# Moving the staging places of the second and fourth group of Q, K, V rows into the third slot of keys

## The chip, the cores and the metric

One core of a Trainium2 chip. The metric is the device time of one execution in microseconds (us), the median of several runs. The engines are TensorE (PE, whose weight loads are shown as PEld), VectorE (DVE), ScalarE (ACT), GpSimd (POOL) and SyncE (SP). SP, ACT and POOL also issue DMA transfers.

## What is computed

A transformer block of 2048 tokens of width 576, attention and feed-forward side by side on the same normalized input:

```python
qkv = (lambda x, *d: x.transpose(*d))((x @ wqkv).reshape(B, S, 3, H, Dh), 2, 0, 3, 1, 4)
...
logits = jnp.einsum("bhsd,bhswd->bhsw", q, kg) * scale
logits = jnp.where(mask[None, None, :, :], logits, -1e9)
attn = _softmax(logits, axis=-1)
o = jnp.einsum("bhsw,bhswd->bhsd", attn, vg)
return (lambda x, *d: x.transpose(*d))(o, 0, 2, 1, 3).reshape(B, S, D) @ wo
...
h = jnp.einsum("bsd,df->bsf", x, w1) + b1
r = jnp.where(h > zero, h, zero)
h = r * r
out = jnp.einsum("bsf,fd->bsd", h, w2) + b2
...
xn = _layernorm(x, axis=-1)
return x + _A_ref(xn, A_wqkv, A_wo) + _B_ref(xn, B_w1, B_b1, B_w2, B_b2)
```

There are 32 heads of 18, and a token attends to 8 places: itself and seven before it, two apart (kg and vg are the keys and values there). The feed-forward goes from 576 to 4608 and back.

## The kernel before

The tokens are four blocks (b = 0 to 3) of 512. All matrix products are in fp32, with each operand split into a high and a low part (ACT copies the high part, DVE subtracts it to get the low one). In order of the program:

- `open_rows` normalizes block 0, turns it and multiplies it by the weights of head group 0 (groups g = 0 to 3, 8 heads each). Four products of 128 tokens ("rows", j = 0 to 3) come out, each 128x432: K, V and Q of one group.
- `q0` computes the 28 remaining rows of blocks 0 and 1, in the order (0,1), (0,3), (0,2), (1,3), (1,2), (1,1), (1,0) as (block, group), four rows each. **Row r** below is the r-th of these, r = 0 to 27. Rows 0 to 25 run here, the last two inside the next stage. Between rows, `run(pieces, k)` issues pieces of other work: statistics and normalization of block 1 (`normalize`), the sums of blocks for the fast matrix scheme of the feed-forward (`sums`), the splitting of the next groups' weights (`split_wq`), small left-over weights (`left_w`, with the ACT copy L589), and then steps of attention (`side`).
- `phase_a(0)` begins the feed-forward of blocks 0 and 1. Its first product (L676) needs the first half of the first weights, which ACT copies (`w1_hi`, L514) and DVE finishes (`w1_lo`), after DVE has combined them (`combine_w1`). Then feed-forward, the rows of blocks 2 and 3, and the second feed-forward follow.

**A row's way.** `qkv_row` (L361 on) takes PSUM bank r % 5, PE multiplies 14 times (L365), and `qkv_out` (L356 on) has ACT copy the bank into a place of the staging tile `st` (L357); ACT itself then issues the transfer of the place to a buffer in DRAM (`kvq`, L359). `st` has four places, one for each j, so row r copies into the place of row r-4, and the copy waits until that row's transfer has landed.

**Slots of keys.** A pool called `kv` has three buffers ("slots"), taken in rotation; a tile waits until the last user of its slot is done. At the start they hold the rows of block 0, the rows of block 1 and the normalized rows. Then attention's keys and values live there: `fetch` (L374 on) loads them when `free[0]`, the count of free slots, exceeds `kept_back[0]`. Here one slot is kept back while the keys and values of (0,0) are loaded after row 6, and given after row 17 to `load_left_x(0, ...)`: two small loads on SP (L599) of left-over inputs. Behind them in SP's queue stand three loads of second weights (`load_w2`, L535) and the next first weights (`load_w1`, L499, L501).

**Order.** The program is written out by hand; each engine executes its own instructions in that order. A DMA instruction whose counters have not been reached holds up everything behind it on the issuing engine. Eight counters (DMAHW0 to 7 below) are raised when transfers of SP and ACT land; they are handed out in turn, and a transfer that gets a counter waits until the one that had it before has landed.

Of the kernel before, what the change touches and what calls it, by code (L numbers as in the profile page):

```python
# [11 lines left out]
AF = mybir.ActivationFunctionType  # L12
# [9 lines left out]
NJ = TB // P  # L22
# [5 lines left out]
CG = HG * DH  # L28
QW = 3 * CG
# [21 lines left out]
def block_kernel(ctx: ExitStack, tc: tile.TileContext, x, xt, wqkv, wo, w1, b1, w2, b2, w1l, out):  # L51
    nc = tc.nc
# [12 lines left out]
    def kv_tile(n):  # L65
        return sb.tile([P, n], F32, name="kv", bufs=3)
# [47 lines left out]
    def bank(i):  # L114
        return ps.tile([P, TB], F32, name=f"p{i}")
# [53 lines left out]
    def statistics(b):  # L169
        mr = sb.tile([P, 2, NJ], F32, name="mr")  # L170
        for j in range(NJ):
            for k in range(2):
                if b == 1:
                    bn_stats(b, rows_of[b], j, k)
                else:
                    if k == 0:
                        ln[b, j] = sb.tile([P, 2, 6], F32, name="st6", bufs=NJ)
                    nc.vector.bn_stats(out=ln[b, j][:, k], in_=rows_of[b][j][:, 0, k * 288:(k + 1) * 288])
            mean_var(b, j)
            nc.vector.tensor_copy(mr[:, 0, j:j + 1], ln[b, j][:, 0:1])  # L180
            inverse_std(mr[:, 1, j:j + 1], ln[b, j][:, 1:2])
            if j == NJ - 1:
                if b > 1:
                    nc.gpsimd.dma_start(mrscr[b].rearrange("n p -> p n"), mr.rearrange("p k j -> p (k j)"))
                mrs[b] = mr
                measured.add(b)
                if b == 1:
                    release()
            yield
# [12 lines left out]
    def turn_mr(b, i):  # L202
        y = bank(i)
        nc.tensor.transpose(y[:2 * NJ, :P], mrs[b].rearrange("p k j -> p (k j)"), ident)
        t = sb.tile([2 * NJ, P], F32, name="mrt")
        nc.scalar.activation(t, y[:2 * NJ, :P], AF.Copy)
        nc.sync.dma_start(mrscr[b], t)

    def load_mb(b):
        assert b in measured  # L210
        mb[b] = (sb.tile([P, 2, TB], F32, name="mb") if b < 3 else
                 sb.tile([P, 2 * NS * P], F32, name="st")[:, :2 * TB].rearrange("p (k t) -> p k t", k=2))
        nc.sync.dma_start(mb[b].rearrange("c k t -> c (k t)"), flat(mrscr[b], 0, [0, P], 2 * NJ * P))
# [13 lines left out]
    def normalize(b):  # L227
        open_x(b)
        for a in (0, 2):
            v = xm[b][:, a:a + 2]  # L230
            for k, op in enumerate((ALU.subtract, ALU.mult)):
                tt(v, v, mb[b][:, k:k + 1].to_broadcast([P, 2, TB]), op)
                if k:
                    soon(lambda v=v, a=a: nc.scalar.activation(X[b][:, 0, a:a + 2], v, AF.Copy))
                yield
        for k, op in enumerate((ALU.subtract, ALU.mult)):
            tt(xf[b], xf[b], mb[b][:, k], op)
        nc.sync.dma_start(xlscr[b], xf[b][:2 * L])
        soon(lambda: left_hi(x4[b], xf[b]))
        yield  # L240
        for a in (0, 2):
            flush()
            tt(X[b][:, 1, a:a + 2], xm[b][:, a:a + 2], X[b][:, 0, a:a + 2].bitcast(F32), ALU.subtract)
            yield
        flush()
        left_lo(x4[b], xf[b])
        normed.add(b)
        yield
# [60 lines left out]
    def load_wq(g, ks=range(3)):  # L309
        for k in ks:  # L310
            n = 2 if k < 2 else 1
            r = raws[g, k] = sb.tile([P, 2, QW], F32, name="r4", bufs=4)[:, :n]
            nc.sync.dma_start(r, wqkv[g, :, 2 * k:2 * k + n])
# [14 lines left out]
    def split_wq(g, name, then=lambda: None):  # L328
        open_wq(g, name)
        for k in range(4):  # L330
            if k < 3:
                wq_hi(g, k)
            if k:
                wq_lo(g, k - 1)
                if k == 3:
                    then()
                    split_up.add(g)
                yield

    qp, stage = {}, {}  # L340

    def row_products(b, g, j):
        js = slice(j * P, (j + 1) * P)
        mm = []
        for c in range(NC):
            w = wq[g, c // 2][:, c % 2]
            if c < NC - 1:
                mm += [(X[b][:, 0, c, js], w[:, 0]), (X[b][:, 1, c, js], w[:, 0]), (X[b][:, 0, c, js], w[:, 1])]
            else:
                mm += [(x4[b][:, js], w[:, 0]), (x4[b][:, js], w[:, 1])]  # L350
        return mm
# [1 line left out]
    def open_stage():  # L353
        stage[0] = sb.tile([P, 2 * NS * P], F32, name="st")[:, :NJ * QW].rearrange("p (j c) -> p j c", c=QW)

    def qkv_out(b, g, j, p):  # L356
        nc.scalar.activation(stage[0][:, j], p[:, :QW], AF.Copy)  # L357
        to = kvq[g][:, PAD + b * TB:PAD + (b + 1) * TB].rearrange("i (p j) c -> p j i c", j=NJ)[:, j]
        nc.scalar.dma_start(to, stage[0][:, j].rearrange("p (i c) -> p i c", c=CG))  # L359

    def qkv_row(b, g, j, i):  # L361
        p = bank(i)
        mm = row_products(b, g, j)
        for k, (l, r) in enumerate(mm):
            nc.tensor.matmul(p[:, :QW], l, r, start=k == 0, stop=k == len(mm) - 1)  # L365
        qkv_out(b, g, j, p)

    def shifted(t, j, *dims):
        a = t[:, j:j + 1, 0:1]
# [2 lines left out]
    loads, landed, queue, free, lane, kept_back = [], {}, [], [0], [nc.sync], [0]  # L372
# [21 lines left out]
    def offer(b, g=None):  # L394
        if g is None:
            loads.append(("x", b, None))
            queue.append((("x", b), lambda: statistics(b)))
        else:
            loads.extend([("k", b, g), ("v", b, g)])
            queue.append((("k", b, g), lambda: attention(b, g)))  # L400
        fetch()
# [77 lines left out]
    def run(gens, k):  # L479

        flush()
        while k > 0 and gens:
            try:
                next(gens[0])
                k -= 1
            except StopIteration:
                gens.pop(0)
        side(k)
# [134 lines left out]
    def load_left_w(i, v):  # L623
        rv["w", i] = v
        nc.sync.dma_start(v[:, :4], w1l[i])
# [687 lines left out]
    def run_all(gens):  # L1313
        while gens:
            run(gens, 1)
# [239 lines left out]
    def q0():  # L1555
        todo = [(b, g, j) for b, g in ((0, 1), (0, 3), (0, 2), (1, 3), (1, 2), (1, 1), (1, 0)) for j in range(NJ)]
        pieces = [statistics(1), split_wq(3, "S")]

        waiting = []

        def row(r):
            b, g, j = todo[r]
            while b and b not in normed or g not in split_up:
                run(pieces, 1)
            qkv_row(b, g, j, r % 5)
            if j == NJ - 1:
                def go(b=b, g=g):
                    offer(b, g)

                if r < 6:  # L1570
                    waiting.append(go)
                else:
                    go()

        for r in range(len(todo) - 2):
            row(r)
            if r == 2:
                turn_mr(1, 7)
                run_all(pieces)
                load_wq(2)  # L1580
                load_mb(1)
            if r == 1:
                load_left_w(0, sb.tile([P, 2 * NS, P], F32, name="w1r", bufs=2))
            if r == 4:
                pieces += [split_wq(2, "h", lambda: load_wq(0)), normalize(1), left_w(0)]
            if r == 6:
                offer(0, 0)
                for late in waiting:
                    late()
                waiting.clear()  # L1590
                lane[0] = nc.gpsimd
            if r == 11:
                run_all(pieces)
                load_w1(0)
            if r == 13:
                pieces.append(sums(0))
            if r == 17:
                free[0] -= 1
                kept_back[0] = 0
                load_left_x(0, kv_tile(2 * NS * P).rearrange("p (s t) -> p s t", t=P))  # L1600
            if r == 19:
                split_up.discard(0)
                pieces.insert(0, split_wq(0, "h"))
            if r == 21:
                run_all(pieces)
                for n in range(3):
                    load_w2(n)
                combine_w1(0)
                load_w1(1)
            if r in (23, 24):  # L1610
                w1_hi(0, r - 23)
                w1_lo(0, r - 23)
            elif r not in (3, 22):
                run(pieces, 3 if r < 1 or 14 <= r < 20 else 1 if r > 20 else 2)

        def filler(i):
            if i < 2:
                row(len(todo) - 2 + i)
            if i == 1:
                last_sum(0)  # L1620

        return filler
# [73 lines left out]
```

## Time and profile before

| | |
|---|---|
| median of 3 runs | 1102.7 us (1102.13 to 1104.84) |
| the profiled execution's own time | 1102.89 us |
| its span, first to last instruction | 1101.2 us |
| PE busy | 1093.1 us, 99% |
| DVE, ACT, POOL busy | 879.5, 562.2, 149.0 us |
| granted TensorE clock | 1.000 |

The times are one execution's, in us from the span's start. In rows of the timeline the columns are: start, duration, engine, line, operation, output<-input, shape, count, and in brackets the idle time just ahead and what the profile takes to have ended it. "ACTq" and "SPq" are DMA instructions on those engines' queues. Matmul ends are modelled, so their starts are the better measure.

### The profile page before, as it was taken

To read this page: it belongs to the slowest core of one execution; us is meant where nothing else is said; L and a number is where in the kernel's file an instruction comes from. 1 tells how busy PE (TensorE), PEld (TensorE's weight loads), DVE (VectorE), ACT (ScalarE), POOL (GpSimd) and SP (SyncE) were. 2 spreads that over 40 slices of the span, in tenths; PEclk is the share of its full clock that TensorE was granted. 3 is DMA by queue.
4 is the path that set the end of the run, shared out by engine and by line. 5 is a ranking of instruction groups with operands and counts; after the bars stand their busy time and mean duration, and the time that the engine had idled before them with its cause. 6 is when DMAs were issued, how large, how long until landed. Compare 5 with 4: busy or idle time off the path is not lost.

```text
span 1101.2 us, 13948 instructions
## 1 busy us (share of the span) xinstructions
PE 1093.1 (99%) x4936; PEld 923.2 (84%) x4936; DVE 879.5 (80%) x1183; ACT 562.2 (51%) x794; POOL 149.0 (14%) x267
## 2 busy tenths in 40 slices
PE   9999999999999999999999999999999999999998
PEld 7998888888888888888899988888888888888887
DVE  7596988899898978999879387776767676889955
ACT  5435766656566654555344345454554545543432
POOL 4000401022030101003010300201101010101010
PEclk9999999999999999999999999999999999999999
DMA  7956998879989887869565988868686877685572
GB/s 278 329 188 233 344 384 320 330 269 272 377 328 299 301 331 255 299 233 328 201 212 164 305 313 300 299 232 318 215 304 210 293 241 298 219 291 190 184 284 88
DMA packets 109558, 298.97 MB, mean 271 GB/s; under 512 B 12648, under 2 KB 42736, under 8 KB 98608
## 3 DMA queue, kind: packets, MB, share of 16 engines
q1 hardware_dynamic: 69984, 192.84, 49.8%
q0 software_dynamic: 13200, 62.52, 16.0%
q10 hardware_dynamic: 26304, 42.71, 11.8%
q8 instruction: 39, 0.64, 0.2%
q14 instruction: 31, 0.25, 0.1%
HBM read 213.53 MB, written 84.50 MB: 271 GB/s over the span
## 4 chain that ended last, share of the span: by engine, by line
PE 94%; DVE 3%; DMA 1%; issue 1%; ACT 1%; ACTq 0%; POOL 0%; DVEq 0%; POOLq 0%
PE p L572 47%; PE p L676 35%; PE p L1102 6%; PE p L365 3%; PE p L1106 1%; PE p L1471 1%; DMA kvq<-st 1%; PE p L682 1%; DVE w1r L118 1%; DVE pr L118 0%; PE p L1388 0%; DVE r L118 0%; DVE S L118 0%; DVE w1s L118 0%; ACT st L357 0%
## 5 line engine op out<-in xcount | busy, mean ns | idle before, releaser
L572 PE MATMUL p<-h,w2s 128*128 128x512 f32 x2066 | 491.3, 389 | 0.1
L572 PEld LDWEIGHTS p<-h,w2s 128*128 128x128 f32 x2066 | 387.5, 188 | 81.4 <-ACT h L722 0.6
L676 PE MATMUL p<-X,w1s 128*128 128x512 f32 x864 | 219.6, 389 | 2.1 <-DVE w1s L118 1.3
L676 PEld LDWEIGHTS p<-X,w1s 128*128 128x128 f32 x864 | 162.0, 188 | 36.3 <-DVE w1s L118 1.7
L545 ACT ACTIVATE w2s<-w2r 128x640 fp32r<-128x640 f32 x164 | 120.2, 735 | 126.5 <-PE p L572 102.1
L118 DVE TENSOR_TENSOR w2s<-w2r,w2s 128x576 fp32r<-128x576 f32 x164 | 123.5, 753 | 72.4 <-ACT w2s L545 72.1
L676 PE MATMUL p<-S,w1s 128*128 128x512 f32 x648 | 164.5, 389 | 0.0
L676 PEld LDWEIGHTS p<-S,w1s 128*128 128x128 f32 x648 | 121.5, 188 | 25.2
L443 POOL DMA_DIRECT2D o<-q x128 | 69.3, 609 | 416.7 <-DVE q L118 415.1
L718 ACT ACTIVATE r<-r,b1t 128x512 f32<-128x512 f32 x72 | 52.2, 725 | 116.4 <-DVE r L118 115.4
L414 DVE TENSOR_REDUCE lg<-pr 128x64 f32<-128x1152 f32 x64 | 86.5, 1351 | 1.2
L118 DVE TENSOR_TENSOR pr<-lg,kv 128x1152 f32<-128x1152 f32 x64 | 86.7, 1354 | 1.0
L118 DVE TENSOR_TENSOR pr<-q,kv 128x1152 f32<-128x1152 f32 x64 | 86.6, 1354 | 0.9
L118 DVE TENSOR_TENSOR pr<-pr 128x576 f32<-128x576 f32 (+1 forms) x128 | 77.6, 606 | 3.5
L118 DVE TENSOR_TENSOR r<-p,r 128x512 f32<-128x512 f32 (+1 forms) x77 | 53.1, 689 | 32.8 <-ACT r L784 15.3
L726 ACT ACTIVATE r<-r 128x1024 f32<-128x1024 f32 x72 | 76.1, 1057 | 1.2
L118 DVE TENSOR_TENSOR h<-r,h 128x1024 fp32r<-128x1024 f32 (+3 forms) x46 | 51.7, 1135 | 23.2 <-ACT r L726 14.9
L760 ACT ACTIVATE r<-p 128x512 f32<-128x512 f32 x36 | 21.5, 598 | 81.8 <-PE p L676 81.8
L118 DVE TENSOR_TENSOR w1s<-w1r,w1s 128x1024 fp32r<-128x1024 f32 (+2 forms) x42 | 46.2, 1104 | 10.2 <-ACT w1s L514 9.5
L718 ACT ACTIVATE r<-p,b1t 128x512 f32<-128x512 f32 x72 | 48.2, 671 | 0.6 <-DMA out<-r 0.4
L118 DVE TENSOR_TENSOR w1r<-w1r 128x256 f32<-128x256 f32 (+5 forms) x69 | 40.8, 591 | 8.0 <-ACT w1r L589 6.4
L118 DVE TENSOR_TENSOR h<-h 128x1024 fp32r<-128x1024 f32 x36 | 43.9, 1220 | 1.8 <-ACT h L999 1.7
(206 smaller groups left out, 1171.6 us busy)
## 6 DMA issues: line engine op xcount, KB each, us to landing
w2r<-in_w SPq DMA_DIRECT2D x144, 320.0 KB, 4.0
kv<-kvq POOLq DMA_DIRECT2D x30, 1296.0 KB, 8.2
w<-w1s SPq DMA_DIRECT2D x21, 1024.0 KB, 7.8
w1s<-w ACTq DMA_DIRECT2D x19, 1024.0 KB, 6.1
h<-r SPq DMA_DIRECT2D x36, 512.0 KB, 6.1
h<-h SPq DMA_DIRECT2D x36, 512.0 KB, 4.2
w<-w1s SPq DMA_DIRECT2D x15, 768.0 KB, 10.1
w1s<-w ACTq DMA_DIRECT2D x15, 768.0 KB, 5.5
```

Source lines behind the costliest of these rows:

```text
L118: return nc.vector.tensor_tensor(out=out, in0=a, in1=b, op=op)
L365: nc.tensor.matmul(p[:, :QW], l, r, start=k == 0, stop=k == len(mm) - 1)
L414: nc.vector.tensor_reduce(out=lg[:, j * HG:(j + 1) * HG].rearrange("p a w -> p w a"), in_=pr.rearrange("p w (a d) -> p w a d", d=DH), axis ...
L443: nc.gpsimd.dma_start(rows[:, i], q[i * L:(i + 1) * L, :, a:z])
L545: nc.scalar.activation(w2s[stream[i]][:, :DE], raw2[i], AF.Copy)
L572: nc.tensor.matmul(yp[b][c], v, a, start=c not in yb[b], stop=c in last and c not in [o[0] for o in ops[i + 1:]], skip_group_check=True)
L676: nc.tensor.matmul(to, l, r, start=start and i == 0, stop=i == len(mm) - 1, skip_group_check=True)
L682: nc.tensor.matmul(to, weight(LEFT, k, f), v, start=False, stop=k == 1, skip_group_check=True)
L718: nc.scalar.activation(to, a, AF.Relu, bias=b1t[:, f:f + 1])
L726: nc.scalar.activation(r, r, AF.Square)
L760: nc.scalar.activation(u[:, 0], bb, AF.Copy)
L1102: nc.tensor.matmul(to, l[:, js], r, start=start and n == 0, stop=n == len(mm) - 1, skip_group_check=True)
```

## The change

Rows 4 to 7 and 12 to 15 (the second and the fourth group of `q0`) use four other places. They lie in a tile taken from the `kv` pool ahead of row 4, the slot that was kept back. The count of free slots falls there and no longer after row 17; `load_left_x` after row 17 takes the next tile of the pool without a count, which in rotation is the slot of the new places. From row 16 on, all rows use the old four places.

```diff
-    def qkv_out(b, g, j, p):
-        nc.scalar.activation(stage[0][:, j], p[:, :QW], AF.Copy)
+    def qkv_out(b, g, j, p, places=0):
+        st = stage[places][:, j]
+        nc.scalar.activation(st, p[:, :QW], AF.Copy)
         to = kvq[g][:, PAD + b * TB:PAD + (b + 1) * TB].rearrange("i (p j) c -> p j i c", j=NJ)[:, j]
-        nc.scalar.dma_start(to, stage[0][:, j].rearrange("p (i c) -> p i c", c=CG))
-
-    def qkv_row(b, g, j, i):
+        nc.scalar.dma_start(to, st.rearrange("p (i c) -> p i c", c=CG))
+
+    def qkv_row(b, g, j, i, places):
         p = bank(i)
         mm = row_products(b, g, j)
         for k, (l, r) in enumerate(mm):
             nc.tensor.matmul(p[:, :QW], l, r, start=k == 0, stop=k == len(mm) - 1)
-        qkv_out(b, g, j, p)
+        qkv_out(b, g, j, p, places)
...
-            qkv_row(b, g, j, r % 5)
+            qkv_row(b, g, j, r % 5, r // NJ % 2 if r < 4 * NJ else 0)
...
         for r in range(len(todo) - 2):
+            if r == NJ:
+                free[0] -= 1
+                kept_back[0] = 0
+                stage[1] = kv_tile(NJ * QW).rearrange("p (j c) -> p j c", c=QW)
             row(r)
...
             if r == 17:
-                free[0] -= 1
-                kept_back[0] = 0
                 load_left_x(0, kv_tile(2 * NS * P).rearrange("p (s t) -> p s t", t=P))
```

Where it moves waits, the built programs show it. On ACT, from row 8's copy on (the first line) to row 11's; p_664 and so on are the rows' PSUM banks, and the names in brackets are what an instruction waits for. Before:

```order
L357 ACTIVATE st<-p_664 128x432 [waits PE_49]
L359 DMA kvq_98<-st 128x3x144 [waits DMAHW7_49,Activation_49]
L357 ACTIVATE st<-p_683 128x432 [waits PE_49]
L359 DMA kvq_98<-st 128x3x144 [waits DMAHW0_49,Activation_49]
L357 ACTIVATE st<-p_705 128x432 [waits DMAHW4_49,PE_49]
L359 DMA kvq_98<-st 128x3x144 [waits DMAHW1_49,Activation_49]
L589 ACTIVATE w1r<-w1r 128x896 [waits DMAHW3_49,DVE_49]
L357 ACTIVATE st<-p_726 128x432 [waits DMAHW5_49,PE_49]
```

And with the change (L357, L359 and L589 are L358, L360 and L590 there):

```order
L358 ACTIVATE st<-p_665 128x432 [waits PE_49]
L360 DMA kvq_98<-st 128x3x144 [waits DMAHW7_49,Activation_49]
L358 ACTIVATE st<-p_684 128x432 [waits PE_49]
L360 DMA kvq_98<-st 128x3x144 [waits DMAHW0_49,Activation_49]
L358 ACTIVATE st<-p_706 128x432 [waits PE_49]
L360 DMA kvq_98<-st 128x3x144 [waits DMAHW1_49,Activation_49]
L590 ACTIVATE w1r<-w1r 128x896 [waits DMAHW3_49,DVE_49]
L358 ACTIVATE st<-p_727 128x432 [waits DMAHW2_49,PE_49]
```

Row 10's copy (p_705, now p_706) no longer waits for a transfer, which was that of row 6, and row 11's waits for that of row 3 and no longer for that of row 7. No instruction has changed its place.

On SP, after row 17: the two loads of `load_left_x`, the three loads of second weights, the next first weights. Before:

```order
L599 DMA kv<-xl_147 128x2x128 [waits DMAHW1_49]
L599 DMA kv<-xl_148 128x2x128
L535 DMA w2r<-in_w 128x640 [waits DMAHW3_49]
L535 DMA w2r<-in_w 128x640
L535 DMA w2r<-in_w 128x640 [waits DMAHW1_49,DVE_49]
L499 DMA w1r<-in_w 128x1024 [waits DMAHW2_49]
L501 DMA w1r<-in_w 128x256 [waits DMAHW4_49]
```

And with the change:

```order
L600 DMA kv<-xl_147 128x2x128 [waits DMAHW2_49,DMAHW3_49,DMAHW1_49,DMAHW5_49,DMAHW0_49,Activation_49]
L600 DMA kv<-xl_148 128x2x128
L536 DMA w2r<-in_w 128x640
L536 DMA w2r<-in_w 128x640 [waits DMAHW6_49]
L536 DMA w2r<-in_w 128x640 [waits DVE_49]
L500 DMA w1r<-in_w 128x1024
L502 DMA w1r<-in_w 128x256 [waits DMAHW4_49]
```

The first load now waits for row 15's copy and for the transfers of rows 12 to 15 (counters 5, 0, 1 and 2), and the loads' own counters are handed out differently.

On ACT, from row 17's copy (p_862) over row 18's (p_890) to row 19's copy and transfer (p_912). Before:

```order
L357 ACTIVATE st<-p_862 128x432 [waits PE_49]
L359 DMA kvq_98<-st 128x3x144 [waits DMAHW0_49,Activation_49]
L357 ACTIVATE st<-p_890 128x432 [waits DMAHW5_49,PE_49]
L359 DMA kvq_98<-st 128x3x144 [waits DMAHW3_49,Activation_49]
L423 ACTIVATE lg<-lg 128x256 [waits DVE_49]
L357 ACTIVATE st<-p_912 128x432 [waits DMAHW6_49,PE_49]
L359 DMA kvq_98<-st 128x3x144 [waits Activation_49]
```

And with the change:

```order
L358 ACTIVATE st<-p_863 128x432 [waits PE_49]
L360 DMA kvq_98<-st 128x3x144 [waits DMAHW0_49,Activation_49]
L358 ACTIVATE st<-p_891 128x432 [waits PE_49]
L360 DMA kvq_98<-st 128x3x144 [waits DMAHW3_49,Activation_49]
L424 ACTIVATE lg<-lg 128x256 [waits DVE_49]
L358 ACTIVATE st<-p_913 128x432 [waits PE_49]
L360 DMA kvq_98<-st 128x3x144 [waits DMAHW5_49,Activation_49]
```

Row 18's transfer waits for counter 3 as before, but that counter's last holder is now the first load of `load_left_x` (it was the first load of second weights); row 19's transfer newly waits for counter 5, now held by the first load of second weights. L423 is the exponential of attention.

## The prediction

> **What bounds the kernel now.** I read the page first, then what PE waited for, then the timeline backwards from those waits.
>
> ```profile
> span 1101.2 us, 13948 instructions
> PE 1093.1 (99%) x4936; PEld 923.2 (84%) x4936; DVE 879.5 (80%) x1183; ACT 562.2 (51%) x794; POOL 149.0 (14%) x267
> ```
>
> PE is busy for all but 8.1 us of the span. Its whole list of waits is three rows long (total, times, longest):
>
> ```profile
> PE p L1388 <- DVE lg L1381: 2.1, 1, 2.1
> PE p L676 <- DVE w1s L118: 1.3, 1, 1.3
> PE p L676 <- ACT w1s L514: 0.8, 1, 0.8
> ```
>
> The first is the start of the program, ahead of the change. The other two lie at one place, where the rows of `q0` end and the feed-forward begins. So the question is whether the change reaches that place. The timeline of PE there:
>
> ```profile
> 89.71 2.52 PE L365 MATMUL p<-h,X 128*128 128x432 f32 x12
> 92.07 0.55 PE L365 MATMUL p<-h,x 128*128 128x432 f32 x2
> 93.42 0.73 PE L676 MATMUL p<-X,w1s 128*128 128x512 f32 x2 [0.80 <-ACT w1s L514]
> 95.43 1.20 PE L676 MATMUL p<-X,w1s 128*128 128x512 f32 x4 [1.28 <-DVE w1s L118]
> 96.47 0.40 PE L742 MATMUL p<-X,w1s 128*128 128x512 f32 x1
> 96.70 1.53 PE L676 MATMUL p<-S,w1s 128*128 128x512 f32 x6
> 98.07 2.52 PE L365 MATMUL p<-h,X 128*128 128x432 f32 x12
> ```
>
> Twelve matmuls of a row take 2.36 from start to start (89.71 to 92.07), so two take 0.39, and the feed-forward could begin at 92.07 + 0.39 = 92.46. Six matmuls of 512 take 1.37 (96.70 to 98.07), so L742 could begin at 93.83. It begins at 96.47. **2.64 us are lost here**: 2.08 as the two waits, the rest in the steps around them. That is the most the change can win, since PE waits for nothing after it.
>
> Why are those weights late? Backwards on ACT and DVE:
>
> ```profile
> 54.40 0.53 ACT L357 ACTIVATE st<-p 128x432 f32<-128x432 f32 x1 [5.08 <-DMA kvq<-st]
> 55.43 0.95 ACT L589 ACTIVATE w1r<-w1r 128x896 fp32r<-128x896 f32 x1 [0.50 <-ACT st L357]
> 56.41 1.09 DVE L118 TENSOR_TENSOR w1r<-w1r 128x896 fp32r<-128x896 f32 x1 [6.44 <-ACT w1r L589]
> ...
> 83.40 0.43 DVE L118 TENSOR_TENSOR lg<-lg,mx 128x256 f32<-128x256 f32 x1
> 83.86 0.42 ACT L423 ACTIVATE lg<-lg 128x256 f32<-128x256 f32 x1 [4.84 <-DMA kvq<-st]
> ...
> 86.10 2.55 DVE L118 TENSOR_TENSOR h<-r,h 128x864 fp32r<-128x864 f32 x3 [2.27 <-ACT h L323]
> ...
> 92.31 1.06 ACT L514 ACTIVATE w1s<-w1r 128x1024 fp32r<-128x1024 f32 x1 [1.16 <-DVE w1r L118]
> 94.16 2.38 DVE L118 TENSOR_TENSOR w1s<-w1r,w1s 128x1024 fp32r<-128x1024 f32 x2
> ```
>
> ACT's L514 at 92.31 waits for DVE's combination of the first weights. DVE gets there late because its work runs in one line from 56.41, with hardly a pause (from 70 to 80 it is busy for 9.13 of 10 us, in a row below): at 83.83 it hands over to ACT (exponential at 83.86, row 19's copy, the weight copies) and takes over again at 86.10. The profile puts the exponential's wait down to a transfer, but its input ends at 83.40 + 0.43 = 83.83, and the order shows that it waits for DVE alone. At 56.41 DVE had been idle for 6.44, waiting for L589. And L589 stood in ACT's queue behind **row 10's copy, which waited 5.08 for row 6's transfer**. That is the wait which the order shows as gone.
>
> **The change, part by part.** No instruction is added; the counts on every engine are the same.
>
> *Row 10's copy.* It starts when PE is done with its bank. How soon, row 9 shows:
>
> ```profile
> 48.20 0.55 PE L365 MATMUL p<-h,x 128*128 128x432 f32 x2
> 48.79 0.53 ACT L357 ACTIVATE st<-p 128x432 f32<-128x432 f32 x1 [2.03 <-PE p L365]
> 50.94 0.56 PE L365 MATMUL p<-h,x 128*128 128x432 f32 x2
> ```
>
> Row 9's copy began 0.04 after its bank's end (48.75). Row 10's bank ends at 51.50, so its copy can begin at 51.54 in place of 54.40: **2.86 earlier**. L589 follows 1.03 later as now, and DVE takes up its work at 53.55 in place of 56.41. What DVE reads next are the keys:
>
> ```profile
> kv<-kvq SPq DMA_DIRECT2D x1, 1296.0 KB, 9.3
> kvq<-st ACTq DMA_DIRECT2D x1, 216.0 KB, 13.2
> ...
> 40.94 0.80 SPq L387 DMA_DIRECT2D kv<-kvq  x2
> 41.13 0.37 ACTq L359 DMA_DIRECT2D kvq<-st  x1
> ```
>
> The first load of keys lands 9.3 after its issue, at 50.2, ahead of 54.64 when DVE will want it. (Row 6's transfer, issued at 41.13 beside those loads, took 13.2: that is row 10's wait.)
>
> *On the way from 53.55 to the combination* one step is held by PE and not by DVE: the first copy of `sums` overwrites weights that row 15 still reads.
>
> ```profile
> 62.30 2.50 PE L365 MATMUL p<-S,X 128*128 128x432 f32 x12
> 65.57 1.06 ACT L271 ACTIVATE S<-w1r 128x1024 fp32r<-128x1024 f32 x1 [5.28 <-DVE w1r L118]
> 67.91 1.22 DVE L118 TENSOR_TENSOR S<-w1r,S 128x1024 fp32r<-128x1024 f32 x1
> ```
>
> Row 15 is through with the first six of its twelve products at 62.30 + 1.18 = 63.48. So this copy ends near 64.6, and DVE wants it at 67.91 - 2.86 = 65.05. It fits with 0.4 to spare, and the whole line moves by 2.86.
>
> *At the start of the feed-forward.* L514 then begins at 89.45 and ends ahead of 92.46. DVE's low part lets the third matmul go at 95.43 - 2.86 = 92.57, and PE wants it after two matmuls, at 92.46 + 0.46 = 92.92. So with a shift x the win is x up to 2.64; with 2.86 it is **all of 2.64**, with 0.3 to spare. PE then has the rest of its work without a wait, so all of it reaches the end.
>
> *Row 11's copy* loses its wait for row 7's transfer likewise, but ran behind row 10's; rows 12 and 13 were waiting for PE. They add nothing to the sum.
>
> *The wait that is added.* `load_left_x` took its slot at once; now SP holds it until row 15's transfer has landed, and the second weights and next first weights stand behind it.
>
> ```profile
> 62.24 0.94 SPq L599 DMA_DIRECT2D kv<-xl  x2
> 63.22 15.43 SPq L535 DMA_DIRECT2D w2r<-in_w  x3
> ...
> 99.25 1.26 DVE L118 TENSOR_TENSOR kv<-kv 128x128 f32<-128x128 f32 x4
> 101.99 0.74 ACT L545 ACTIVATE w2s<-w2r 128x640 fp32r<-128x640 f32 x1 [0.44 <-ACT st L357]
> ...
> 70.00:80.00 10.00, 10.00 (x53) 9.62 (x52) 9.13 (x10) 3.06 (x5) 0.00 (x0) 1.00 0.25 67
> ...
> kvq<-st ACTq DMA_DIRECT2D x1, 216.0 KB, 3.7
> kv<-xl SPq DMA_DIRECT2D x1, 128.0 KB, 3.9
> ```
>
> Row 15's bank ends at 62.30 + 2.36 + 0.55 = 65.2; its copy follows the second copy of `sums` at about 66.2, its transfer leaves at 66.8 and, with the 3.7 of row 14's in this stretch, lands near 70.5. SP's loads then leave 8 us later than now. Their users come at 99.25 and 101.99, and the third load of second weights stood until 63.22 + 15.43 = 78.65 anyway, for DVE. The transfers move into a stretch where the DMA engines are busy a quarter of the time (0.25). What it costs beside that: row 18's transfer, which stands ahead of the exponential, may only leave once the first of these loads has landed, at 70.5 + 3.9 = 74.4. The exponential waits for DVE until 83.83 - 2.86 = 80.97, so nothing, with 6 us to spare. From below the cost is nothing, because nobody waits for these loads early; from above, row 6's 13.2 stands for 3.7.
>
> The Trainium skill, "DMA: Bandwidth & Descriptors", section "Queues, rings and completion order", says that the write which raises a counter lands only after every earlier write of the same DMA engine, across its queues. The trace agrees: row 6's 216 KB, issued on ACT's queue among SP's loads of keys, took 13.2 us and row 14's 3.7. By that rule row 15's landing depends on what else is in flight, which is the mechanism of the slower case below; with little in flight, as above, the sum stays 2.64.
>
> **The sum.** The profiled execution took 1102.89 with a span of 1101.2. Less 2.64: a span of 1098.56 and a time of 1100.25. The profiled execution lies 0.19 above the median of 1102.7, so the median becomes 1100.06, say **1100.1 us** (-0.24%).
>
> **The rivals.**
>
> *A part of it (1101.3).* ACT must copy row 23 before L514, and that copy waits for row 19's transfer, with keys being loaded beside it:
>
> ```profile
> 84.73 0.37 ACTq L359 DMA_DIRECT2D kvq<-st  x1
> 90.62 0.53 ACT L357 ACTIVATE st<-p 128x432 f32<-128x432 f32 x1 [0.81 <-DMA kvq<-st]
> ```
>
> It is in place from 84.73 to 90.6. Moved by 2.86 it would be issued at 81.87 and be ready near 87.8. If the keys of the next group, loaded by POOL from 81.62 (78.8 then), hold it to 90.6 all the same, L514 begins at 91.65, its end (92.7) starts DVE's low part, and the third matmul goes at about 94.05 (half of the 2.38 and the hand-overs): a win of 95.43 - 94.05 = 1.4. Against it: it needs 8.7 us where the trace has 5.9 here; for it: row 6's 13.2.
>
> *Slower (1103.7).* Row 15's transfer takes 13.2 and lands at 80.0; the first load of `load_left_x` lands with its 3.9 near 84, and row 18's transfer holds ACT until then. With its issue (0.4) and a hand-over the exponential comes near 84.8 and not at 83.86, and PE is about 1 us later than now. It decides only if that load lands after 83.8. Against it: between 70 and 80 the DMA engines are busy a quarter of the time, so nothing as large as the keys is in flight.
>
> *More (1099.5).* The last small wait of the first feed-forward steps, at 115, goes too:
>
> ```profile
> PEld p L572 <- ACT h L722: 0.6, 1, 0.6
> ```
>
> That would be 0.6 on top. But ACT's L722 follows from PE's own products a few us before, so it moves along with PE.
>
> *No effect (1102.7).* The added places do nothing if another wait stands behind row 10's; the order shows only PE's for it.
>
> **How the numbers follow.** Forecast 0.74, part 0.12, more 0.05, no effect 0.05, slower 0.04. The range of 8 in 10 goes from 1099.3 (more, or the runs' scatter, as the lowest run of 1102.13 lies 0.6 below the median) to 1102.0 (over the part's 1101.3 by as much). A measurement of this kernel tells about 0.3%, 3.3 us, from no change. The forecast's 2.64 stays within it; only "more" and scatter pass 1099.4: faster 0.12; slower by as much 0.03, beyond the slower case's own price; same 0.85.
>
> **What would show it.** In the profile after: row 10's copy near 51.5 without a transfer's name; DVE's first attention product near 54.6; L599 on SP near 70.5; the exponential near 81.0; L514 near 89.4; no wait at L676; L742 near 93.8; a span near 1098.5. If L742 moved by less than DVE's work, the part is right; if row 18's transfer stands behind L599, the slower case.

## The result and the profile after

The changed kernel takes **1100.19 us** (median of 10 runs, 1099.64 to 1101.1), the kernel before 1102.56 in runs beside it; the ratio is 0.9976, interval 0.9966 to 0.9985. The gain is clear of the scatter, though smaller than 0.3%. The ratio is taken over all the runs, so it can differ a little from that of the two medians. The page of the changed kernel and its whole list of PE's waits:

```profile
span 1098.5 us, 13947 instructions
PE 1092.3 (99%) x4936; PEld 922.9 (84%) x4936; DVE 879.9 (80%) x1183; ACT 563.2 (51%) x794; POOL 149.3 (14%) x267
```

```profile
PE p L1389 <- DVE lg L1382: 2.1, 1, 2.1
PE p L573 <- ACT h L723: 0.2, 1, 0.2
```

The two waits for the first weights are gone. (Lines below L355 have moved by one or more: L357 is L358, L514 is L515, L589 is L590, L742 is L743.) PE where the feed-forward begins:

```profile
91.75 0.55 PE L366 MATMUL p<-h,x 128*128 128x432 f32 x2
92.13 1.52 PE L677 MATMUL p<-X,w1s 128*128 128x512 f32 x6
93.49 0.39 PE L743 MATMUL p<-X,w1s 128*128 128x512 f32 x1
```

By the prediction's own measure nothing is lost: 93.49 - (91.75 + 0.39 + 1.37) = -0.02, where it was 2.64. The way there, on ACT and DVE:

```profile
51.21 0.53 ACT L358 ACTIVATE st<-p 128x432 f32<-128x432 f32 x1 [2.22 <-PE p L366]
52.24 0.95 ACT L590 ACTIVATE w1r<-w1r 128x896 fp32r<-128x896 f32 x1 [0.50 <-DMA kv<-kvq]
53.23 1.09 DVE L118 TENSOR_TENSOR w1r<-w1r 128x896 fp32r<-128x896 f32 x1 [3.29 <-ACT w1r L590]
54.24 1.35 DVE L118 TENSOR_TENSOR pr<-q,kv 128x1152 f32<-128x1152 f32 x1
63.35 1.06 ACT L271 ACTIVATE S<-w1r 128x1024 fp32r<-128x1024 f32 x1 [3.39 <-PE p L366]
64.73 1.22 DVE L118 TENSOR_TENSOR S<-w1r,S 128x1024 fp32r<-128x1024 f32 x1
...
80.68 0.42 ACT L424 ACTIVATE lg<-lg 128x256 f32<-128x256 f32 x1 [4.89 <-DMA kvq<-st]
...
89.13 1.06 ACT L515 ACTIVATE w1s<-w1r 128x1024 fp32r<-128x1024 f32 x1 [1.47 <-DVE w1r L118]
90.98 2.39 DVE L118 TENSOR_TENSOR w1s<-w1r,w1s 128x1024 fp32r<-128x1024 f32 x2
```

Row 10's copy (51.21) waits for PE alone. DVE's steps stand 3.18 ahead of their time before (the first 56.41 to 53.23, the last 94.16 to 90.98). The copy at 63.35 is only 2.22 ahead, since row 15's products hold it, but it still ends before DVE wants it. 0.33 of the 3.18 is not the change: this execution ran ahead by that much already at row 9 (48.79 before, 48.46 now). The rest, 2.85, is row 10's shift.

### The profile page after: what moved, and what is told of

It reads as the page before. It is cut to its first block, busy times and chain, and to the rows that moved or that the text cites. A ratio compares the mean times of both kernels' runs of the same rounds, so it can differ in the third digit from the quotient of the medians.

```text
span 1098.5 us, 13947 instructions
## 1 busy us (share of the span) xinstructions
PE 1092.3 (99%) x4936; PEld 922.9 (84%) x4936; DVE 879.9 (80%) x1183; ACT 563.2 (51%) x794; POOL 149.3 (14%) x267
## 4 chain that ended last, share of the span: by engine, by line
PE 99%; DVE 0%; ACT 0%; issue 0%; POOL 0%; ACTq 0%; POOLq 0%
PE p L573 47%; PE p L677 35%; PE p L366 7%; PE p L1103 6%; PE p L1107 1%; PE p L1472 1%; PE p L683 1%; PE p L1389 0%; PE p L1434 0%; DVE w1s L118 0%; ACT X L122 0%; PE p L1371 0%; ACT h L723 0%; DVE w2s L118 0%; DVE r L118 0%
## 5 line engine op out<-in xcount | busy, mean ns | idle before, releaser
L573 PE MATMUL p<-w1s,w2s 128*128 128x512 f32 x195 | 44.7, 389 | 0.0
```

The lines of the kernel that those rows point to most:

```text
L573: nc.tensor.matmul(yp[b][c], v, a, start=c not in yb[b], stop=c in last and c not in [o[0] for o in ops[i + 1:]], skip_group_check=True)
```

## The experiments

Theory A is the prediction's: row 10's copy waits for row 6's transfer, L589 waits behind it, DVE's line begins late, PE lacks the first weights. Theory B: the other copies' waits and the counters dealt out anew carry part of the win. Theory C: the win comes from the loads on SP that leave 9 us later. Each kernel was run beside the kernel before on the same chip. The series ran on several chips, so the ratio, and not the median alone, is what compares one experiment with another.

### Parts of the change

Only the second group, only the fourth, row 6 alone, and all but row 6. The edit is the condition for the new places:

```diff
-            qkv_row(b, g, j, r % 5, r // NJ % 2 if r < 4 * NJ else 0)
+            qkv_row(b, g, j, r % 5, 1 if NJ <= r < 2 * NJ else 0)
```

> Only rows 4 to 7 use the new places; rows 12 to 15 stay in the old ones. Theory A (row 10's copy, through L589 and DVE's line, is the whole cause): all of the win, 1100.2 us, span 1098.5, no wait of PE at the first product of the feed-forward. Theory B (the waits of rows 11 to 15 and the counters handed out anew carry part of it): between 1100.6 and 1102.2. Theory C (the loads of left-over inputs and second weights, which leave 9 us later, carry it): the first of those loads waits here for row 7 alone, which is long done, so it leaves at once again and the win is gone, 1102.6.

Measured: 1100.19 us, ratio 0.9983 (0.9974 to 0.9992), span 1098.4. The timeline of SP and PE:

```profile
59.21 0.90 SPq L600 DMA_DIRECT2D kv<-xl  x2
```

```profile
91.67 0.54 PE L366 MATMUL p<-h,x 128*128 128x432 f32 x2
...
93.42 0.39 PE L743 MATMUL p<-X,w1s 128*128 128x512 f32 x1
```

PE could begin at 91.67 + 0.39 here, so by the measure above nothing is lost. All of the win is there as far as the runs can tell (1.94 against this series' 1102.13, and the interval overlaps the change's), with the loads on SP leaving at 59.21 and not at 71. That speaks against theory C, and the fourth group's new places add nothing that these runs show.

```diff
-            qkv_row(b, g, j, r % 5, r // NJ % 2 if r < 4 * NJ else 0)
+            qkv_row(b, g, j, r % 5, 1 if 3 * NJ <= r < 4 * NJ else 0)
```

> Only rows 12 to 15 use the new places; row 10 waits for row 6's transfer again. Theory A: no win, 1102.6 us, row 10's copy near 54, 2.6 us lost at the first product of the feed-forward. Theory B: part of the win, 1100.6 to 1102.2. Theory C: the first of the moved loads waits for row 15 as in the change, so all of the win, 1100.2.

Measured: 1102.09 us against 1102.13 in the same series, ratio 1.0005 (0.9996 to 1.0014): no win. The timelines of ACT, SP and PE:

```profile
53.80 0.53 ACT L358 ACTIVATE st<-p 128x432 f32<-128x432 f32 x1 [4.59 <-DMA kvq<-st]
...
71.56 0.89 SPq L600 DMA_DIRECT2D kv<-xl  x2
...
92.83 0.74 PE L677 MATMUL p<-X,w1s 128*128 128x512 f32 x2 [0.32 <-ACT w1s L515]
94.83 1.20 PE L677 MATMUL p<-X,w1s 128*128 128x512 f32 x4 [1.27 <-DVE w1s L118]
```

The loads leave late here (71.56) and the waits at the first product stand: theory C is out.

```diff
-            qkv_row(b, g, j, r % 5, r // NJ % 2 if r < 4 * NJ else 0)
+            qkv_row(b, g, j, r % 5, 1 if r == 6 else 0)
```

> One row, row 6, uses a new place; all others the old ones, so row 11 waits for row 7's transfer (landed near 54.9) and rows 12 and 13 for theirs. Theory A: all of the win, 1100.2 us, since row 11's copy stands behind L589. Theory B: 1101 or more. Theory C: 1102.6.

Measured: 1100.6 us, ratio 0.9987 (0.9979 to 0.9996); row 10's copy at 51.44, and L743 again 1.75 behind the start of the row's last two matmuls (91.97), as in the change (1.74):

```profile
91.97 0.55 PE L366 MATMUL p<-h,x 128*128 128x432 f32 x2
...
93.72 0.39 PE L743 MATMUL p<-X,w1s 128*128 128x512 f32 x1
```

One place does it at this spot of the program, so theory B is not needed. Four of its eleven runs lie between 1101.5 and 1102.8, so its ratio is a little weaker than the change's; the intervals overlap.

```diff
-            qkv_row(b, g, j, r % 5, r // NJ % 2 if r < 4 * NJ else 0)
+            qkv_row(b, g, j, r % 5, r // NJ % 2 if r < 4 * NJ and r != 6 else 0)
```

> The change, but row 6 stays in its old place, so row 10 waits for its transfer. Theory A: nothing of the win, 1102.6 us, with L589 near 55.4 and a wait of some 2 us at the first product. Theory B: most of the win, below 1101.5. Theory C: all of it, 1100.2.

Measured: median 1103.81 us with runs from 1101.35 to 1105.5, ratio 1.0008 (0.9998 to 1.0018): no win, although every other wait is moved as in the change. So theory B is out. (The median is 1.7 above its series' 1102.13. That is not explained; the last section tells of a lower granted clock that four of the eleven runs have.) Its profiled execution (1101.74):

```profile
52.51 0.53 ACT L358 ACTIVATE st<-p 128x432 f32<-128x432 f32 x1 [3.73 <-DMA kvq<-st]
53.54 0.95 ACT L590 ACTIVATE w1r<-w1r 128x896 fp32r<-128x896 f32 x1 [0.50 <-ACT st L358]
54.53 1.09 DVE L118 TENSOR_TENSOR w1r<-w1r 128x896 fp32r<-128x896 f32 x1 [4.84 <-ACT w1r L590]
...
93.54 1.20 PE L677 MATMUL p<-X,w1s 128*128 128x512 f32 x4 [1.01 <-DVE w1s L118]
```

Row 6's transfer took 11.8 here and not 13.2; row 10 waited 3.73 in place of 5.08, and PE waited 1.0 in place of 2.1. So the loss is not the same in every execution.

### The same win without new places

In the kernel before, only L589 is moved ahead of row 10's copy:

```diff
+            if r == 10:
+                run(pieces, 1)
             row(r)
...
-                run(pieces, 3 if r < 1 or 14 <= r < 20 else 1 if r > 20 else 2)
+                run(pieces, 3 if r < 1 or 14 <= r < 20 else 1 if r > 20 or r == 10 else 2)
```

> The kernel before, without any new place; only L589, the ACT copy of the left-over weights, is issued ahead of row 10's copy and no longer behind it. Row 10 still waits for row 6's transfer. Theory A (what matters is DVE's start behind L589): all of the win, 1100.2 us or a few tenths more, DVE's attention products from about 52, and no wait at the first product of the feed-forward. Theory D (row 10's late bank or the transfers themselves matter, and L589 only stands in their queue): no win, 1102.6.

Measured: 1100.28 us, ratio 0.9981 (0.9973 to 0.999). The timelines of ACT, DVE and PE:

```profile
49.50 0.95 ACT L589 ACTIVATE w1r<-w1r 128x896 fp32r<-128x896 f32 x1 [0.68 <-DVE w1r L118]
50.49 1.09 DVE L118 TENSOR_TENSOR w1r<-w1r 128x896 fp32r<-128x896 f32 x1 [1.02 <-ACT w1r L589]
53.03 0.53 ACT L357 ACTIVATE st<-p 128x432 f32<-128x432 f32 x1 [2.58 <-DMA kvq<-st]
...
91.96 1.55 PE L676 MATMUL p<-X,w1s 128*128 128x512 f32 x6
...
672.45 0.73 PE L682 MATMUL p<-x,w1s 128*128 128x512 f32 x2 [1.44 <-DMA w1s<-w]
```

Row 10 still waits for its transfer (2.58), and PE still does not wait at 91.96. So row 10's copy is not what hurts; L589 behind it is. Theory D, that row 10's late bank or the transfers themselves do the harm, falls. (The profiled execution took 1102.52, for a reason far away: at 672 PE waited 1.44 for a load of the second feed-forward's weights.)

### The dose

In the changed kernel, L589 is done three and five times:

```diff
-    def high_low(v, store):
+    def high_low(v, store, times=1):
...
-        nc.scalar.activation(hi.bitcast(F32R), lo, AF.Copy)
+        for _ in range(times):
+            nc.scalar.activation(hi.bitcast(F32R), lo, AF.Copy)
...
-            dims(lwscr[i], k * L * NS * P, [NS * P, L], [2 * L * NS * P, G], [1, NS * P]), part.rearrange("p s c -> p (s c)")))
+            dims(lwscr[i], k * L * NS * P, [NS * P, L], [2 * L * NS * P, G], [1, NS * P]), part.rearrange("p s c -> p (s c)")), 3 if i == 0 else 1)
```

> The changed kernel with L589 done three times in a row (the same result; two copies of 0.95 us more on ACT). Theory A: the shift of DVE's line falls from 2.86 to about 0.96, and the win with it, 1101.6 us, with a wait of 1.5 to 1.7 at the first product. If DVE's line has slack: still 1100.2.

Measured: 1102.1 us, ratio 0.9997 (0.9988 to 1.0005): most of the win is gone. A win of 1.0 was expected to stay, and 0.3 is left by the ratio, with an interval that reaches to 1.3. In the profiled execution the third matmul goes 1.00 earlier than before (94.43 for 95.43):

```profile
55.42 1.09 DVE L118 TENSOR_TENSOR w1r<-w1r 128x896 fp32r<-128x896 f32 x1 [4.80 <-ACT w1r L591]
...
92.43 0.73 PE L678 MATMUL p<-X,w1s 128*128 128x512 f32 x2
94.43 1.20 PE L678 MATMUL p<-X,w1s 128*128 128x512 f32 x4 [1.27 <-DVE w1s L118]
```

> The changed kernel with L589 done five times (four copies, 3.8 us more on ACT). Theory A: DVE's line begins 0.95 later than in the kernel before, so it is slower than before, 1103.5 us. If slack takes it up: 1102.6 or less.

Measured: 1104.11 us, ratio 1.0016 (1.0005 to 1.0028): slower than before, as expected, though by more than the 0.9 expected.

```profile
56.90 1.09 DVE L118 TENSOR_TENSOR w1r<-w1r 128x896 fp32r<-128x896 f32 x1 [7.53 <-ACT w1r L591]
...
87.70 2.22 PE L366 MATMUL p<-h,X 128*128 128x432 f32 x10 [0.42 <-DVE h L118]
...
95.92 1.20 PE L678 MATMUL p<-X,w1s 128*128 128x512 f32 x4 [1.27 <-DVE w1s L118]
```

Here a second wait appears ahead of the first product: row 24 waits for its own weights (87.70), which DVE splits in the same line. DVE's line begins 0.49 later than before, and the third matmul goes 0.49 later (95.92 for 95.43). That is about a third of the 1.7 by which the median rose; where the rest comes from is not shown.

Beside each other, the start of DVE's line and of the third matmul of the first product:

| kernel | DVE's line begins | third matmul | difference |
|---|---|---|---|
| before | 56.41 | 95.43 | 39.02 |
| fourth group only | 55.81 | 94.83 | 39.02 |
| all but row 6 | 54.53 | 93.54 | 39.01 |
| L589 three times | 55.42 | 94.43 | 39.01 |
| L589 five times | 56.90 | 95.92 | 39.02 |

In five executions of five kernels the third matmul follows the start of DVE's line by 39.0 us. By that rule the change would let it go at 53.23 + 39.02 = 92.25, ahead of PE, which reaches it at 92.13 + 0.46 = 92.59: PE sets the time again.

The size fits too. What DVE's line gains on PE, less what PE itself ran ahead in that execution (the start of row 24's last two matmuls, 92.07 before), is what the loss of 2.64 falls by:

| kernel | DVE's line earlier by | PE ahead by | difference | loss | falls by |
|---|---|---|---|---|---|
| fourth group only | 0.60 | 0.10 | 0.50 | 2.14 | 0.50 |
| all but row 6 | 1.88 | 0.53 | 1.35 | 1.28 | 1.36 |
| L589 three times | 0.99 | 0.10 | 0.89 | 1.74 | 0.90 |

### The cap

The change, with L589 ahead of row 10 too (the edit of the kernel with the same win, made in the changed one).

> The changed kernel, and L589 (there L590) ahead of row 10's copy as well, so DVE's line begins some 5 us earlier than before the change, until the copy held by row 15's products lets about 3.2 of it through. Theory A with its cap (PE can take no more than the 2.64 lost at the first product): the same as the change, 1100.2 us, span near 1098.5. If the win goes on growing with the shift: 1099.5 or less.

Measured: 1100.41 us, span 1098.9, ratio 0.9967 (0.9954 to 0.998): the same time as the change. The timelines of ACT and DVE:

```profile
63.61 1.06 ACT L271 ACTIVATE S<-w1r 128x1024 fp32r<-128x1024 f32 x1 [3.40 <-PE p L366]
...
64.70 1.23 DVE L118 TENSOR_TENSOR S<-w1r,S 128x1024 fp32r<-128x1024 f32 x1 [1.92 <-ACT S L271]
...
89.11 1.07 ACT L515 ACTIVATE w1s<-w1r 128x1024 fp32r<-128x1024 f32 x1 [1.47 <-DVE w1r L118]
```

DVE's line began at 51.20, 2 us ahead of the change's, and gave it back as an idle 1.92 at 64.70, where the copy is held by row 15's products: this is the step that the prediction named as held by PE. L515 then began at 89.11, as in the change (89.13). So the larger shift never reached the first product, and this run does not try whether PE could take more than 2.64 there. The change itself speaks for that cap: its loss is -0.02, with 0.34 to spare (92.25 for 92.59).

### What row 6's transfer waits for

In the kernel before, the load of the values of block 0, group 0 is issued after row 11:

```diff
             if r == 6:
+                kept_back[0] = 2
                 offer(0, 0)
...
                 load_w1(0)
+                kept_back[0], lane[0] = 1, nc.sync
+                fetch()
+                lane[0] = nc.gpsimd
```

> The kernel before, without new places; the load of the values of block 0, group 0 (1296 KB), which are not needed before 89 us, is issued behind the first weights, after row 11, and no longer beside row 6's transfer. If row 6's landing of 13.2 us comes from the loads of keys and values in flight: it lands by about 50, row 10's copy comes near 51.5 to 52, and with theory A the win is 2.2 to 2.6, 1100.0 to 1100.4 us. If the 13.2 has another cause (its own queue, its small pieces): row 10 waits as before, 1102.6. If the moved load gets in the way of the first weights or of later rows: above 1102.6.

Measured: 1101.23 us, ratio 0.9985 (0.9976 to 0.9993). Row 6's transfer and row 10's copy:

```profile
kvq<-st ACTq DMA_DIRECT2D x1, 216.0 KB, 8.8
```

```profile
51.56 0.53 ACT L357 ACTIVATE st<-p 128x432 f32<-128x432 f32 x1 [2.22 <-PE p L365]
```

With one load of 1296 KB in flight and not two, row 6's transfer takes 8.8 us in place of 13.2, row 10 waits for PE alone, and PE has no wait at the first product. So its landing does depend on the loads in flight. Whether it shares the DMA engines' time with them, or its counter's write has to wait for theirs, these runs do not tell apart; the prediction took the 13.2 as agreeing with the second, and it fits either. The median is 1 us above the change's; in the profiled execution (1101.5) PE waits 1.0 far behind, at 967, for the outputs of block 2:

```profile
PE p L572 <- DVE S L979: 1.0, 1, 1.0
```

The moved load is not needed for this wait: row 6 alone and all but row 6, which move no load, show it with 0.5. What sets its length is not shown.

### The price of the added wait

The change, with rows 16 to 19 in the new places too, and the loads of left-over inputs behind row 19:

```diff
-            qkv_row(b, g, j, r % 5, r // NJ % 2 if r < 4 * NJ else 0)
+            qkv_row(b, g, j, r % 5, 1 if NJ <= r < 2 * NJ or 3 * NJ <= r < 5 * NJ else 0)
...
-            if r == 17:
+            if r == 19:
                 load_left_x(0, kv_tile(2 * NS * P).rearrange("p (s t) -> p s t", t=P))
```

> The changed kernel, and rows 16 to 19 use the new places too, with the loads of left-over inputs behind row 19: SP waits until row 19's transfer has landed, near 85.7, in place of 71. Second weights and next first weights stand behind it as before. Theory of the prediction (the added wait costs nothing as long as its loads land before their users at 94 to 99, and as long as the row transfers that take over their counters are not held): 1100.2 us, at most 0.9 more, since row 22's transfer may leave only when the first of these loads has landed (88 to 89.6). Rival (the added wait has a price that grows with it): 1102 or more.

Measured: 1101.05 us (1100.02 to 1103.12), ratio 0.998 (0.9968 to 0.9993). The timelines of SP and ACT:

```profile
85.92 0.89 SPq L600 DMA_DIRECT2D kv<-xl  x2
```

```profile
88.91 0.37 ACTq L360 DMA_DIRECT2D kvq<-st  x1
89.32 0.53 ACT L358 ACTIVATE st<-p 128x432 f32<-128x432 f32 x1 [2.38 <-DMA kv<-xl]
89.88 0.37 ACTq L360 DMA_DIRECT2D kvq<-st  x1
90.30 1.06 ACT L515 ACTIVATE w1s<-w1r 128x1024 fp32r<-128x1024 f32 x1 [0.44 <-DVE w1r L118]
```

This is the mechanism of the prediction's slower case at work: row 22's transfer holds ACT for 2.38 until the load whose counter it takes over has landed. In the profiled execution (1100.52) it still costs PE nothing: L515 ends at 91.36, just as DVE is free for its half (91.39), and PE begins at 92.46 without a wait. But the slack is nearly gone. In the change L515 had ended at 90.19, 0.8 before DVE came to its half at 90.98; here there is none, so a later landing would delay DVE at once, and PE some 0.3 later. The median is 0.6 above that of the change with L589 ahead, run in the same series, but the intervals overlap, so a price is not shown. That the upper runs are executions with a later landing is argued.

## Why the prediction was right

- **The bound.** That PE loses 2.64 at one place, and that the rest runs on without that loss, held: the loss there is -0.02 now, the span fell by 2.7, the median by 2.37. (L743 came 2.98 earlier, the 0.33 of lead included; the lead was given back further along.) By the ratio the step is 2.6, with 1.7 to 3.7 in the interval, so that 1100.19 came within 0.1 of the forecast is in part luck. What the prediction took no account of is that row 6's landing, and with it the loss, changes from execution to execution: 2.64 in the kernel before, profiled once, 2.14 and 1.28 in the two kernels above that keep row 10's wait. So a median of the kernel before need not hold the 2.64 of its profile. The prediction also put the least difference that a measurement can tell at 0.3%; the interval here reaches 0.1% to either side.
- **Row 10's copy.** Forecast at 51.54, 2.86 earlier; found at 51.21 with 0.33 of lead from before, so 2.86 by the change. L589, DVE's start and the keys followed as worked out. That this one wait is the cause was shown from both sides: row 6 alone has the win, all but row 6 has not.
- **One line of DVE.** It passed the whole shift on; the five equal differences of 39.0 show how rigid it is. That ends only where it meets the copy held by row 15, as with the start at 51.20. The copy held by PE was forecast to end near 64.6 and DVE to want it at 65.05. It ended at 64.41 for 64.73.
- **The cap.** A start of DVE's line 2 us earlier still brought the same time (1100.41), because the copy held by row 15 let no more through. The 2.64 as a limit of its own rests on the prediction's sum and on the change's loss of nothing.
- **The exponential's wait.** The profile again names a transfer (80.68, idle 4.89). It came 3.18 earlier, with all the rest of DVE's line: reading its wait as DVE's was right.
- **The added wait.** Row 15's transfer and SP's loads of left-over inputs, by the time from issue to landing (the last number, in us):

```profile
kvq<-kv ACTq DMA_DIRECT2D x1, 216.0 KB, 4.1
kv<-xl SPq DMA_DIRECT2D x2, 128.0 KB, 2.3
```

And SP's timeline behind its wait:

```profile
71.09 0.89 SPq L600 DMA_DIRECT2D kv<-xl  x2
72.04 3.44 SPq L536 DMA_DIRECT2D w2r<-in_w  x3
```

The row's transfer took 4.1 where 3.7 was assumed, the loads left at 71.09 where 70.5 was forecast, and landed in 2.3 where 3.9 was assumed. Nothing was late for them. The longer version, in which they leave some 15 us later still, shows where a price would come in: at a row's transfer on ACT that takes over a load's counter.

- **The rivals.** "A part" needed row 19's transfer to take 8.7; row 23's copy came at 87.13, 5.6 after that transfer was issued (81.55), and the profile names PE for its wait and no transfer. "More" did not happen: a wait of 0.2 for L723 stayed with PE. "Slower" and "no effect" are out.

## What to carry to other kernels

A wait that costs an engine 5 us may matter only through what stands behind it in that engine's queue: look for the small instruction that another, busy engine needs, and either end the wait or issue that instruction ahead of it; both gave the same time here. Before pricing such a win, work out where it is capped (here the 2.64 that PE lost at one product), and which later steps let no more than a part of the shift through: above that it comes back as idle time further along, as DVE's 1.92 did. And when a buffer's wait moves to another queue, ask which transfers stand behind it and which of the shared landing counters they hold.

## What was not expected

Some executions of nearly every kernel here lie 2 us above the rest, and the profiles of two kernels show a late wait of PE of 1 us or more: 1.44 for a load of weights at 672 us, 1.0 for the outputs of block 2 at 967. The changed kernel's ten runs and the twelve of the kernel with both edits show nothing of it (at most 1101.3). No experiment was made on that, so it stays open whether the other kernels' remaining waits for row transfers have a part in it.

The runs show one thing more. The kernels in which PE waits at the first product (the kernel before in the experiments' three series, the fourth group only, all but row 6, L589 three and five times) have 139 runs. In 20 of them the granted TensorE clock is 0.998 or 0.997 over the whole run, and each of these took 1103.8 us or more. The 79 runs of the kernels without that wait all have 0.999 or 1.000, and none took more than 1103.2. So the removal of the wait seems to take these long runs away as well. Whether a pause of 1 to 3 us brings the lower clock, and how, is not shown: none of those 20 was profiled.
